# Attention, soft routing and a dense expert block in one kernel: new places for the routing steps, head sums added up pair by pair, and two weight blocks loaded during the attention

## The chip, the cores and the metric

One core of a Trainium2 chip runs the whole program in one launch. The metric is the device time in microseconds (us), the median of the runs shown. Engines are named as the profile names them: PE (TensorE; PEld are its weight loads), DVE (VectorE), ACT (ScalarE), POOL (GpSimd), SP (SyncE, which issues all DMAs here, in its program's order).

## What is computed

```python
def reference(q, k, v, phi, w1, w2, w_in, w_out, s, b):
    # 8 batches, 8 heads, 576 positions, head size 64
    scores = q @ k.T / 8, masked by blocks of 64 (a row block sees the blocks up to its own)
    x = (softmax(scores) @ v)                     # as 4608 tokens x 512
    logits = x @ phi                              # phi 512 x 32
    d = softmax of logits over the tokens         # per slot
    slot_input = d.T @ x                          # 32 slots, 4 for each of 8 experts
    slot_out = relu(slot_input[e] @ w1[e]) @ w2[e]    # w1 8x512x1024, w2 8x1024x512
    x = (softmax of logits over the slots) @ slot_out
    return (s * relu(x @ w_in) ** 2 + b) @ w_out  # w_in 512x2048, w_out 2048x512, float64 words
```

## The kernel before

The program has three stages. **Attention** takes 32 pairs of heads (8 batches of 4 pairs), one after the other. For a pair `p`, `rough` computes rounded scores in four parts r0 to r3, and `rough_max` takes from them, on DVE, the row maxima over blocks of 64 keys; `rough_join` joins two maxima of each row and `m_row` turns them into a row that SP copies into `mr`. Then `score` (four chunks s0 to s3) computes the exact scores in PSUM, `expo` the exponentials `pc` (ACT), `key_sum` adds them up into `S` (POOL, on DVE in the last pair), `sum_hi` and `sum_lo` split `S` into two fp16 parts `sh` and `sl`, `pv` multiplies by V, `tokens` turns the result to tokens and multiplies by phi (tile `tp`, with only one buffer), `dens` sums the denominators into the same tile, and `norm` writes the normalised tokens and their part of the logits to `XB` (4 tiles of 128 tokens) and `XT` (the last 64 tokens of a batch).

The score tiles `s` in PSUM form a ring of two: a part of `rough` or a chunk of `score` can be written only when the tile before the last was read by its `expo` or `rough_max`. r3 of the next pair shares the tile of s1, and the two readers of that tile, `expo` of chunk 1 and `rough_max` of r3, wait for each other in program order.

After each fourth pair a **routing** of the batch runs between the steps of the next pair. `route_s0` sums the logits of the eight heads (the helper `head_sum`, a reduction on DVE), `route_p` transposes them (PE) and takes their running maximum, `route_l` exponentiates (ACT), `route_e` transposes back, `route_x` multiplies by the tokens and adds to `acc`. All of these share `tp` with `tokens`, which waits for the last of them. The last batch's routing has nothing beside it; `slot_inputs` then writes `slotT`.

The **expert stage** multiplies by w1 and w2, 32 blocks of 1 MB each loaded in two halves of 512 KB (`load_w`). Its blocks lie in ten places: four `wlate` and four `wpost` in the memory that the attention's tiles leave, two `wright` in that of the routing's tiles. A place is loaded anew when `used` tells that its block was multiplied. Beside it DVE and ACT convert `w_out` from 64-bit words (`split_wo`). The **dense stage** follows, and the change does not touch it.

What sets the order of the work in the first two stages is the table `SLOT`: each step of a pair has a time in units of an eighth of a pair, every step is put into the plan at `8 * p` plus that time, and the sorted plan is written out engine by engine. So a number of the table decides only which instructions stand before which on an engine's queue. V tiles `RV` have three buffers and are loaded some two pairs ahead (`ld_v`).

Of the kernel before, what the change touches and what calls it, by code (L numbers as in the profile page):

```python
# [10 lines left out]
F32 = mybir.dt.float32  # L11
# [23 lines left out]
}  # L35

ON = {"k": "A", "q": "A", "sl": "D"}
# [6 lines left out]
def fused_kernel(  # L44
# [34 lines left out]
    wpre = wholes(ctx, "wpre", NPRE)  # L79

# [12 lines left out]
    wt = {}  # L93

# [48 lines left out]
    XB = rtp.tile([128, 4, 8, 96], F32, name="xb", bufs=1)  # L143
    XT = rtp.tile([128, 8, 96], F32, name="xt", bufs=1)
# [9 lines left out]
    KT, QT, RV = [None] * 3, [None] * 3, [None] * 3  # L154
    for i in (2, 0, 1):
        KT[i] = earlyp.tile([128, 640], F32, name=f"kt_{i}")
        QT[i] = earlyp.tile([128, 640], F32, name=f"qt_{i}")
        RV[i] = earlyp.tile([128, 5, 128], F32, name=f"rv_{i}")
# [3 lines left out]
    NB_ = {"pc": 5, "mT": 4, "ssp": 1}  # L162
# [12 lines left out]
    MM = [latep.tile([128, 2, 5, 2], F32, name=f"mm_{i}") for i in range(2)]  # L175
# [7 lines left out]
    def build_rest():  # L183
        for d in MX:
            POOL.memset(d.bitcast(F32), 0.0)
        for d in MM:
            POOL.memset(d, -3.0e38)
        POOL.memset(EX[32:64, 128:256], 0.0)
# [100 lines left out]
    def rough_max(p, r):  # L289
        ps = st.pop(("rps", p, r))  # L290
        mm, me = MM[p % 2][:, :, :, 0], MM[p % 2][64:128, :, :, 1]
        by64 = ps[64:128].rearrange("p h (u c) -> p h u c", c=64)
# [9 lines left out]
        else:  # L302
            rmax(me[:, :, 0:1], ps[64:128, :, 448:512])

    def rough_join(p):
        rmax(MX[p % 2][:, 0:10], MM[p % 2].rearrange("p h j a -> p (h j) a"))

# [44 lines left out]
    def key_sum(p, c):  # L352
# [4 lines left out]
        if p == NP - 1 and c == 3:  # L357
            sh, sl = st["s3"] = [ring("s" + x, [128, 2, 576], F16)[:, :, 0:256] for x in "hl"]
# [29 lines left out]
    def pv(p, c):  # L388
        if c == 0:
            st["last"] = st["pv", p] = ps_v.tile([128, 2, 512], F32, tag="pv", name="pv")  # L390
        pc, rv = st["pc", p, c], RV[p % 3]
# [42 lines left out]
    def norm(p):  # L434
# [5 lines left out]
        if p == NP - 1:  # L440
# [3 lines left out]
        DVE.tensor_tensor(out=XB[:, :, 2 * j:2 * j + 2, :], in0=ps[:, :, 0:384].rearrange("p h (u c) -> p u h c", u=4),  # L444
                          in1=rr[:, 0:4].to_broadcast([128, 4, 2, 96]), op=ALU.mult)

        DVE.tensor_tensor(out=XT[l0:l0 + 64, 2 * j:2 * j + 2, :], in0=ps[64:128, :, 384:480],
                          in1=rr[64:128, 4].to_broadcast([64, 2, 96]), op=ALU.mult)
# [13 lines left out]
    def head_sum(o, x):  # L462

        DVE.tensor_reduce(out=o, in_=x, axis=AX, op=ALU.add)  # L464

    def route_s0(b, j0=0, j1=8):

        if b == NB - 1:
            n = 0 if j0 == 0 else 1
            if n == 0:  # L470
                st["part"] = [rtp.tile(x, F32, tag=t, name=t, bufs=1)
                              for t, x in (("partx", [128, 4, 32, 2]), ("partt", [128, 32, 2]))]
            w, v = st["part"]
            head_sum(w[:, :, :, n], XB[:, :, j0:j1, 64:96].rearrange("p u h n -> p u n h"))
            head_sum(v[:, :, n], XT[:, j0:j1, 64:96].rearrange("p h n -> p n h"))
            if n == 0:
                return
            g = lgs[:, gt(b):gt(b) + 5, :]
            DVE.tensor_tensor(out=g[:, 0:4], in0=w[:, :, :, 0], in1=w[:, :, :, 1], op=ALU.add)
            DVE.tensor_tensor(out=g[:, 4], in0=v[:, :, 0], in1=v[:, :, 1], op=ALU.add)  # L480
            return
        head_sum(lgs[:, gt(b):gt(b) + 4, :], XB[:, :, :, 64:96].rearrange("p u h n -> p u n h"))
        if b % 2:
            head_sum(lgs[:, gt(b) + 4, :], XT[:, :, 64:96].rearrange("p h n -> p n h"))

# [49 lines left out]
    def route_x(b):  # L535
# [5 lines left out]
        if b % 2:  # L541
            PE.matmul(ps[0:32, :], d[:, 128:160], XT[:, :, 0:64], start=False, stop=True)
# [5 lines left out]
    def route_s(b):  # L548
# [28 lines left out]
    for p in range(NP):  # L577
# [30 lines left out]
        A("norm", norm)  # L608
        A("mr", m_row)
    for b in range(NB):  # L610
        z = 8 * (4 * b + 3) + O["route"]
        if b == NB - 1:
            at(8 * (NP - 1) + O["den"] + 0.001, 8, route_s0, b, 0, 6)
            at(z + O["rh"], 8, route_s0, b, 6, 8)
        else:
            at(z + O["rh"], 8, route_s0, b)
# [643 lines left out]
```

## Time and profile before

| | |
|---|---|
| median of 3 runs (lowest, highest) | 843.72 us (843.55, 844.74) |
| the profiled execution | 841.7 us |
| its span in the profile | 839.9 us |
| busy share of the span: PE, DVE, ACT, POOL | 93%, 81%, 70%, 26% |
| attention and last routing, expert stage, dense stage | up to about 379 us, 379 to 443, 443 to the end |

The profile shows one execution. Its page has, among others, the span cut into 40 slices of 21 us with the busy share of each engine, the clock that TensorE was granted and the share of the DMA engines; the trace behind it gives for each instruction its start, its duration and what it waited for. A chain of waits is followed back from the last instruction and names at each moment the one thing that was being waited for.

### The profile page before, as it was taken

The numbers are of one execution on the slowest core, as the hardware profiler recorded it, in microseconds if no ns is written. First come the engines' busy times: TensorE is split into PE (matmuls) and PEld (weight loads), VectorE is DVE, ScalarE is ACT, GpSimd is POOL, SyncE is SP. The second block draws the span as 40 slices with busy tenths as digits, with TensorE's granted clock in tenths as the row PEclk, the third lists the DMA queues.
The fourth block names the chain that finished last, engine by engine and source line by source line (L and its number), as shares of the span: only waits on it lengthen the run. The fifth ranks groups of instructions, "written<-read, shape, count | busy, mean of one in ns | idle before, by whom it ended". The sixth has DMA issues, their size and how long they took to land.

```text
span 839.9 us, 18427 instructions
## 1 busy us (share of the span) xinstructions
PE 780.2 (93%) x7604; PEld 580.5 (69%) x7604; DVE 681.7 (81%) x1175; ACT 585.3 (70%) x848; POOL 220.2 (26%) x191
## 2 busy tenths in 40 slices
PE   4999989898989899967888889999999999999996
PEld 3666757575667575732314678888888888888885
DVE  5788888888888888669876788888888888888885
ACT  4766767575767666547876787777777877877771
POOL 3553534443535344402000011111111111111110
PEclk9999999999999999988899999999999999999999
DMA  4565543242434433299990000000000000000001
GB/s 144 196 211 181 196 145 96 81 159 101 157 133 146 146 96 96 82 385 407 397 392 9 1 26 27 26 27 26 27 26 27 26 27 26 27 26 27 26 27 51
DMA packets 40483, 92.97 MB, mean 111 GB/s; under 512 B 4624, under 2 KB 4944, under 8 KB 40400
## 3 DMA queue, kind: packets, MB, share of 16 engines
q1 hardware_dynamic: 40400, 91.80, 31.3%
q8 instruction: 60, 0.98, 0.5%
q14 instruction: 23, 0.19, 0.1%
HBM read 81.86 MB, written 9.44 MB: 109 GB/s over the span
## 4 chain that ended last, share of the span: by engine, by line
PE 77%; DVE 10%; DMA 8%; ACT 3%; issue 1%; POOL 1%; SPq 0%; POOLq 0%; DVEq 0%; ACTq 0%
PE s L343 13%; PE o L1121 13%; PE o L1123 12%; PE o L1122 12%; PE pv L397 9%; PE tp L415 4%; DMA w<-in_moe_w_dram 4%; PE s L286 4%; PE h L1084 4%; DMA w2h<-in_moe_w_dram 3%; DVE mm L272 3%; DVE lgs L464 2%; PE tp L428 2%; ACT rhl L1102 1%; PE hp L922 1%
## 5 line engine op out<-in xcount | busy, mean ns | idle before, releaser
L272 DVE TENSOR_REDUCE mm<-s 64x4 f32<-64x256 f32 (+5 forms) x224 | 139.1, 634 | 50.2 <-ACT pc L350 30.1
L1103 DVE TENSOR_TENSOR rhl<-G,rhl 128x1792 f16<-128x1792 f32 (+1 forms) x76 | 146.2, 1923 | 3.1 <-ACT rhl L1102 2.7
L350 ACT ACTIVATE pc<-s 128x896 f32<-128x896 f32 (+1 forms) x128 | 104.0, 838 | 58.7 <-PE s L343 30.4
L1085 ACT ACTIVATE r<-h 128x512 f32<-128x512 f32 x144 | 85.8, 596 | 60.8 <-PE h L1084 60.8
L343 PE MATMUL s<-qt,kt 64*128 64x448 f32 (+4 forms) x768 | 124.5, 416 | 1.2 <-DVE mm L272 0.5
L1102 ACT CAST rhl<-G 128x1792 f16<-128x1792 f32 (+1 forms) x76 | 121.0, 1592 | 5.4 <-DVE G L1095 5.3
L365 POOL TENSOR_TENSOR S<-pc 128x896 f32<-128x896 f32 x31 | 64.9, 2093 | 181.8 <-ACT pc L350 181.8
L1123 PEld LDWEIGHTS <-rhl 128*128 128x128 f16 x1008 | 98.8, 98 | 13.2 <-DVE rhl L1103 1.6
L1121 PEld LDWEIGHTS <-rhl 128*128 128x128 f16 x1008 | 98.8, 98 | 13.2
L1122 PEld LDWEIGHTS <-rhl 128*128 128x128 f16 x1008 | 98.8, 98 | 11.8
L397 PE MATMUL pv<-pc,rv 128*64 128x448 f32 (+4 forms) x768 | 100.3, 397 | 0.0
L371 POOL TENSOR_TENSOR S<-S,pc 128x640 f32<-128x640 f32 (+2 forms) x93 | 93.3, 1003 | 7.3
L343 PE MATMUL s<-mr,neg 64*128 64x448 f32 (+4 forms) x384 | 94.9, 487 | 0.0
L1140 POOL TENSOR_TENSOR z<-u,bdif 128x256 f32<-128x256 f32 x18 | 41.8, 2320 | 188.8 <-DVE u L1126 188.8
L1093 DVE TENSOR_TENSOR G<-G 128x512 f32<-128x512 f32 (+1 forms) x76 | 50.5, 665 | 46.5 <-ACT G L1092 46.0
L1092 ACT ACTIVATE G<-r 128x1024 f32<-128x1024 f32 (+1 forms) x76 | 76.9, 1011 | 2.2
L397 PEld LDWEIGHTS pv<-pc,rv 128*64 128x64 f32 x768 | 47.3, 136 | 32.1 <-issue 20.7
L343 PEld LDWEIGHTS s<-qt,kt 64*128 64x128 f32 x768 | 60.4, 188 | 7.4 <-DVE mm L272 2.9
L286 PE MATMUL s<-kr,qr 64*128 64x64 f32 (+4 forms) x384 | 54.0, 348 | 10.2 <-ACT kr L243 7.9
L286 PEld LDWEIGHTS s<-kr,qr 64*128 64x128 f32 x384 | 32.7, 191 | 40.2 <-ACT pc L350 21.1
L1084 PE MATMUL h<-ct,mst 128*128 128x256 f16 x288 | 55.2, 274 | 3.5 <-DVE mst L1049 1.3
L415 PEld LDWEIGHTS tp<-IP,ot 64*128 64x128 f32 x640 | 40.8, 188 | 17.3 <-ACT kr L243 7.3
(302 smaller groups left out, 1787.9 us busy)
## 6 DMA issues: line engine op xcount, KB each, us to landing
w<-in_moe_w_dram SPq DMA_DIRECT2D x36, 512.0 KB
w2h<-in_moe_w_dram SPq DMA_DIRECT2D x28, 512.0 KB
qt<-in_q_dram SPq DMA_DIRECT2D x32, 320.0 KB
kt<-in_k_dram SPq DMA_DIRECT2D x32, 320.0 KB
rv<-in_v_dram SPq DMA_DIRECT2D x32, 320.0 KB
wi<-in_moe_w_in_dram SPq DMA_DIRECT2D x8, 1024.0 KB
wo<-in_moe_w_out_dram SPq DMA_DIRECT2D x8, 1024.0 KB
out_dram<-ob SPq DMA_DIRECT2D x16, 256.0 KB
```

Of the source, the lines that this page charges most:

```text
L272: DVE.tensor_reduce(out=o, in_=i, axis=AX, op=ALU.max)
L286: PE.matmul(ps[:, h, o:o + k1 - k0], qt[a, 128 * j:128 * j + 128], kt[a, k0:k1], start=(n == 0), stop=(n == len(RG[r]) - 1))
L343: PE.matmul(ps[:, h, o:o + c1 - c0], a[r], b[r], start=(n == 0), stop=(n == 1))
L350: ACT.activation(out=pc[:, :, 0:w], in_=st.pop(("ps", p, c))[:, :, 0:w], func=AF.Exp, scale=scale)
L371: eng.tensor_tensor(out=x, in0=x, in1=pc[:, :, o:o + c1 - c0], op=ALU.add)
L397: PE.matmul(st["pv", p][r, x[0], x[1]], rv[:, sl, r], pc[:, h, o:o + c1 - c0], start=head, stop=(sl == 4 or c1 <= 128))
L1084: PE.matmul(hps[:, 256 * o:256 * o + 256], mst[:, 128 * f:128 * f + 128], ct[g], start=True, stop=True)
L1102: ACT.copy(rh, G)
L1103: DVE.tensor_tensor(out=rl, in0=G, in1=rh, op=ALU.subtract)
L1121: PE.matmul(o, rh[:, a, n], bh, start=first, stop=False)
L1122: PE.matmul(o, rh[:, a, n], bl, start=False, stop=False)
L1123: PE.matmul(o, rl[:, a, n], bh, start=False, stop=last)
```

## The change

Six things are changed together.

1. `rough_max` reduces all 128 rows for the second maximum too (before, the lower 64), and `rough_join` masks the upper half with a constant column and takes the larger of two in one instruction.
2. `head_sum` becomes an addition for each pair: in the second, third and fourth pair of a batch DVE adds the logits of the pair's two heads to `LA`. `route_s0` is then one addition of two halves. `XT` becomes the fifth tile of `XB`.
3. `SLOT` has new numbers. V is loaded one pair ahead, into two buffers.
4. Two places (`wearly`) of their own hold the first two blocks of w1, loaded in the pairs 26 and 27. Only two `wlate` places remain, so there are ten places as before.
5. `keep_busy` issues products of 128x128 that nobody reads, 10, 3 and 3 of them, between the steps of the last routing.
6. The clearing of `slotT` goes from DVE to POOL, and some rings are smaller (`ot`, `mT`, the conversion's tile `ag`).

```diff
 SLOT = {
-    "ld_k": -20.09325, "ld_q": -20.15856, "ld_v": -11.10707, "rd_k": -14.81079, ...
+    "ld_k": -17.68370, "ld_q": -17.95831, "ld_v": 1.95502, "rd_k": -12.42489, ...
...
-    XB = rtp.tile([128, 4, 8, 96], F32, name="xb", bufs=1)
-    XT = rtp.tile([128, 8, 96], F32, name="xt", bufs=1)
+    XB = rtp.tile([128, 5, 8, 96], F32, name="xb", bufs=1)
+    LA = rtp.tile([128, 5, 2, 32], F32, name="la", bufs=1)
...
-    NB_ = {"pc": 5, "mT": 4, "ssp": 1}
+    NB_ = {"pc": 5, "ot": 1}
...
-        t = {"k": KT, "q": QT, "v": RV}[nm][p % 3]
+        t = {"k": KT, "q": QT, "v": RV}[nm][p % (2 if nm == "v" else 3)]
...
-        mm, me = MM[p % 2][:, :, :, 0], MM[p % 2][64:128, :, :, 1]
-        by64 = ps[64:128].rearrange("p h (u c) -> p h u c", c=64)
+        mm, me = MM[p % 2][:, 0], MM[p % 2][:, 1]
+        by64 = ps.rearrange("p h (u c) -> p h u c", c=64)
...
     def rough_join(p):
-        rmax(MX[p % 2][:, 0:10], MM[p % 2].rearrange("p h j a -> p (h j) a"))
+        mm, me = (MM[p % 2][:, n].rearrange("p h j -> p (h j)") for n in range(2))
+        DVE.scalar_tensor_tensor(out=MX[p % 2][:, 0:10], in0=me, scalar=mlow[:, 0:1], in1=mm, op0=ALU.add, op1=ALU.max)
...
-    def head_sum(o, x):
-
-        DVE.tensor_reduce(out=o, in_=x, axis=AX, op=ALU.add)
...
+    def head_sum(p):
+
+        b, j = p // 4, p % 4
+        if j == 0:
             return
...
+        n = 4 + b % 2
+        x = XB[:, 0:n, 2 * j:2 * j + 2, 64:96]
+        eng = {"P": POOL, "D": DVE}["D" if p == NP - 1 else ON["hs"]]
+        eng.tensor_tensor(out=LA[:, 0:n], in0=XB[:, 0:n, 0:2, 64:96] if j == 1 else LA[:, 0:n], in1=x, op=ALU.add)
+
+    def route_s0(b):
+
+        n = 4 + b % 2
+        DVE.tensor_tensor(out=lgs[:, gt(b):gt(b) + n, :], in0=LA[:, 0:n, 0], in1=LA[:, 0:n, 1], op=ALU.add)
...
+    def keep_busy(n):
+
+        ps = rps(NB - 1, True)[:, 1]
+        for _ in range(n):
+            PE.matmul(ps[:, 0:128], idF, idF, start=True, stop=True)
...
+    at(8 * (NP - 1) + O["den"] + 0.0002, 0, keep_busy, 10)
+    at(z + O["rp"] + 0.0002, 9, keep_busy, 3)
+    at(z + O["rx"] + 0.0002, 10, keep_busy, 3)
...
+    early = [split(t) for t in wearly]
+    for i, t in enumerate(early):
+        home["w1", i] = t
+        at(8 * (26 + i), 10, load_w, ("w1", i), t)
...
-    wlate = wholes(ctx, "wlate", 4, reuse_waits="tile")
+    wlate = wearly + wholes(ctx, "wlate", 4 - NEARLY, reuse_waits="tile")
...
-    toload = list(wseq[16:])
+    toload = list(wseq[16 + NEARLY:])
...
-    at(8 * (NP - 1) + O["norm"] + 0.02, 9, DVE.memset, slotT, 0.0)
+    at(8 * (NP - 1) + O["norm"] + 0.02, 9, POOL.memset, slotT, 0.0)
```

The order of the instructions, not their times, at three places. In a row stand the line, the operation, what it writes and reads, and the size of what it writes. The first place is PE's queue in the pair after the second batch (`kr` and `qr` are `rough`'s operands, `lgs` and `ex` the routing's). Before:

```order
L286 MATMUL s<-kr_130,qr_132 128x512 x2
L313 MATMUL tp<-idF,lgs 128x64 x2
L494 MATMUL tp<-idF,lgs 32x64 x2
L397 MATMUL pv<-pc,rv_136 64x448 x2
L397 MATMUL pv<-pc,rv_136 64x320 x2
...
L286 MATMUL s<-kr_130,qr_132 128x320 x2
L313 MATMUL tp<-idF,ex 128x64 x2
L521 MATMUL tp<-idF,ex 128x64
L343 MATMUL s<-qt_138,kt_137 128x448 x2
L343 MATMUL s<-mr_144,neg 128x448 x2
L539 MATMUL tp<-xb,d 32x512 x4
```

The same place in the changed program:

```order
L311 MATMUL s<-kr_136,qr_138 128x512 x2
L424 MATMUL pv<-pc,rv_145 64x448 x2
L339 MATMUL tp<-idF,lgs 128x64 x2
L516 MATMUL tp<-idF,lgs 32x64 x2
L424 MATMUL pv<-pc,rv_145 64x320 x2
...
L339 MATMUL tp<-idF,ex 128x64 x2
L543 MATMUL tp<-idF,ex 128x64
L311 MATMUL s<-kr_136,qr_138 128x192 x2
L311 MATMUL s<-kr_136,qr_138 128x320 x2
L561 MATMUL tp<-xb,d 32x512 x4
L564 MATMUL tp<-xb,d 32x512
```

The transposes of the logits now stand behind chunk 1 of `pv`, those of the exponentials ahead of r2, and `route_x` ahead of s0. Nothing else moves on PE in the attention.

The second place is DVE's queue at the same point. Before (`mm` and `mx` are the row maxima, `mb` and `nrun` the routing's):

```order
L272 TENSOR_REDUCE mm_162<-s 64x2
L439 TENSOR_SCALAR rs_164<-tp 128x10
L443 RECIPROCAL rr<-rs_164 128x10
L444 TENSOR_TENSOR xb<-tp,rr 128x4x192
L447 TENSOR_TENSOR xt<-tp,rr 64x192
L272 TENSOR_REDUCE mx_160<-mm_162 128x10
L464 TENSOR_REDUCE lgs<-xb 128x128
L464 TENSOR_REDUCE lgs<-xt 128x32
L272 TENSOR_REDUCE mm_161<-s 128x2
L272 TENSOR_REDUCE mm_161<-s 64x2x2
L497 TENSOR_REDUCE mb<-tp 128x1
```

And changed (`la` is the running head sum, `ag` and `wi` belong to the conversion of `w_in`):

```order
L297 TENSOR_REDUCE mm_168<-s 128x2
L663 SCALAR_TENSOR_TENSOR ag<-ag,wi_596 128x512
L332 SCALAR_TENSOR_TENSOR mx_166<-mm_168,mlow 128x10
L665 SCALAR_TENSOR_TENSOR wi_596<-wi_596,ag 128x512
L466 TENSOR_SCALAR rs_171<-tp 128x10
...
L479 TENSOR_TENSOR xb<-tp,rr 64x192
L501 TENSOR_TENSOR la<-la,xb 128x320
L297 TENSOR_REDUCE mm_167<-s 128x2
L297 TENSOR_REDUCE mm_167<-s 128x2x2
L506 TENSOR_TENSOR lgs<-la 128x160
L519 TENSOR_REDUCE mb<-tp 128x1
```

The reductions over eight heads are gone. The maximum of r3 and the join stand ahead of the norm, and in half of the pairs both steps of a conversion do too. The addition that completes the logits stands behind the maxima of r1.

The third place is SP's queue at the end of the attention. Before:

```order
L239 DMA rv_142<-in_v_dram 128x640
L107 DMA wo_4565<-in_moe_w_out_dram 128x2x1024
L325 DMA mr_144<-mT 1x5x128 x2
L113 DMA w2h<-in_moe_w_dram 128x1024 x8
L113 DMA w_4_0_4915<-in_moe_w_dram 128x1024
```

And changed:

```order
L351 DMA mr_149<-mT 1x5x128 x2
L126 DMA wo_4556<-in_moe_w_out_dram 128x2x1024
L264 DMA rv_145<-in_v_dram 128x640
L351 DMA mr_150<-mT 1x5x128 x2
L264 DMA rv_148<-in_v_dram 128x640
L132 DMA w2h<-in_moe_w_dram 128x1024 x4
L132 DMA w_4_0_4925<-in_moe_w_dram 128x1024
```

V of the last pair now stands behind the last `mr`, and four halves (two blocks) instead of eight stand ahead of the first `wpost` place, `w_4_0`.

## Rows read from the trace of the kernel before

**Rows 1.** The page's 40 slices: DMA engines' busy share in tenths

```profile
DMA  4565543242434433299990000000000000000001
```

**Rows 2.** Chain of waits, the same step in three pairs: start us, us, what

```profile
309.55 2.10 PE pv L397 x20
...
319.45 2.10 PE pv L397 x20
...
343.20 2.10 PE pv L397 x20
```

**Rows 3.** Waits of PE from 20 to 356 us: us in total, times, longest

```profile
PE tp L313 <- DVE lgs L464: 7.7, 7, 1.1
PE tp L415 <- DVE acc L544: 6.7, 7, 1.0
```

**Rows 4.** Chain of waits in the pair after the seventh batch

```profile
325.18 0.93 ACT pc L350
...
326.13 0.30 DVE mm L272
...
328.45 1.85 DVE lgs L464
...
332.25 1.15 DVE mm L272
...
335.73 0.76 DVE acc L544
...
336.62 1.36 PE tp L415 x20
```

**Rows 5.** DVE, 20 to 356 us, by form: x count | busy us, mean ns

```profile
L258 DVE TENSOR_TENSOR sl<-pc,sh 128x256 f16<-128x256 f32 x31 | 13.2, 426 | 1.3 <-ACT sh L376 1.0
L636 DVE SCALAR_TENSOR_TENSOR ag<-ag,wi 128x512 int32<-128x512 int32 x16 | 10.9, 683 | 0.0
L464 DVE TENSOR_REDUCE lgs<-xt 128x32 f32<-128x256 f32 x3 | 1.8, 596 | 0.0
```

**Rows 6.** POOL, whole span, by form

```profile
L365 POOL TENSOR_TENSOR S<-pc 128x896 f32<-128x896 f32 x31 | 64.9, 2093 | 181.8 <-ACT pc L350 181.8
L371 POOL TENSOR_TENSOR S<-S,pc 128x640 f32<-128x640 f32 x31 | 48.1, 1551 | 2.4
L1140 POOL TENSOR_TENSOR z<-u,bdif 128x256 f32<-128x256 f32 x18 | 41.8, 2320 | 188.8 <-DVE u L1126 188.8
```

**Rows 7.** Instructions in order of time, PE, POOL and DVE in pair 30

```profile
351.32 0.97 PE L397 MATMUL pv<-pc,rv 128*64 128x448 f32 x4
...
352.10 3.22 POOL L371 TENSOR_TENSOR S<-S,pc 128x640 f32<-128x640 f32 x3
353.21 0.71 DVE L258 TENSOR_TENSOR sl<-pc,sh 128x256 f16<-128x256 f32 x1 [1.03 <-ACT sh L376]
```

**Rows 8.** Instructions in order of time, SP at the attention's end

```profile
354.44 1.84 SPq L113 DMA_DIRECT2D w2h<-in_moe_w_dram  x4
363.38 0.80 SPq L113 DMA_DIRECT2D w2h<-in_moe_w_dram  x2
```

**Rows 9.** Chain of waits: last routing, a product for `roots`, the last weights

```profile
366.54 1.02 DVE slotT L676
...
373.73 1.87 PE s L539 x8
...
387.36 0.33 PE roots L820 x2
...
431.91 10.38 DMA w2h<-in_moe_w_dram
```

**Rows 10.** Stretches: PE, PEld, DVE, ACT, POOL busy us; granted clock, DMA share, GB/s

```profile
369.50:370.00 0.50, 0.00 (x0) 0.00 (x0) 0.47 (x3) 0.00 (x0) 0.00 (x0) 0.52 1.03 393
438.00:440.00 2.00, 1.61 (x8) 0.29 (x8) 0.00 (x0) 0.00 (x0) 0.00 (x0) 1.00 1.05 408
```

**Rows 11.** Chain of waits at the start: from a K load's issue to its landing

```profile
7.95 3.24 DMA kt<-in_k_dram
```

More of the change, by code (lines that the diff above doesn't have):

```diff
@@ L93, in fused_kernel, with __init__, __getitem__, tile @@
     wt = {}
+    class split:
+        def __init__(self, pool):
+            self.pool, self.t = pool, None
+        def __getitem__(self, h):
+            if h == 0:
+                self.t = self.pool.tile([128, 2048], F32, tag="w", name="w2h")
+            t = self.t
+            class place:
+                def tile(_, shape, dt, tag, name):
+                    return t[:, 1024 * h:1024 * h + 1024]
+            return place()
     def words(key, q0, q1):
@@ L157, in fused_kernel @@
         QT[i] = earlyp.tile([128, 640], F32, name=f"qt_{i}")
-        RV[i] = earlyp.tile([128, 5, 128], F32, name=f"rv_{i}")
+        if i == 2:
+            AG = earlyp.tile([128, 512], I32, name="ag")
+        else:
+            RV[i] = earlyp.tile([128, 5, 128], F32, name=f"rv_{i}")
     MR = [earlyp.tile([128, 640], F32R, name=f"mr_{i}") for i in range(2)]
@@ L173, in fused_kernel @@
     MX = [latep.tile([128, 128], F32R, name=f"mx_{i}") for i in range(2)]
-    MM = [latep.tile([128, 2, 5, 2], F32, name=f"mm_{i}") for i in range(2)]
+    MM = [latep.tile([128, 2, 2, 5], F32, name=f"mm_{i}") for i in range(2)]
+    mlow = const.tile([128, 1], F32, name="mlow")
     RS = [latep.tile([128, 10], F32, name=f"rs_{i}") for i in range(2)]
@@ L187, in build_rest @@
             POOL.memset(d, -3.0e38)
+        POOL.memset(mlow, 0.0)
+        POOL.memset(mlow[0:64], -3.0e38)
         POOL.memset(EX[32:64, 128:256], 0.0)
@@ L357, in key_sum @@
         if p == NP - 1 and c == 3:
-            sh, sl = st["s3"] = [ring("s" + x, [128, 2, 576], F16)[:, :, 0:256] for x in "hl"]
+            t = ring("S", [128, 2, 448], F32).rearrange("p h c -> p (h c)").bitcast(F16)
+            sh, sl = st["s3"] = [t[:, 512 * x:512 * x + 512].rearrange("p (h c) -> p h c", h=2) for x in range(2)]
             ACT.copy(sh, pc[:, :, 0:256])
@@ L443, in norm @@
         DVE.reciprocal(out=rr.rearrange("p u h a -> p (u h a)"), in_=r)
-        DVE.tensor_tensor(out=XB[:, :, 2 * j:2 * j + 2, :], in0=ps[:, :, 0:384].rearrange("p h (u c) -> p u h c", u=4),
+        DVE.tensor_tensor(out=XB[:, 0:4, 2 * j:2 * j + 2, :], in0=ps[:, :, 0:384].rearrange("p h (u c) -> p u h c", u=4),
                           in1=rr[:, 0:4].to_broadcast([128, 4, 2, 96]), op=ALU.mult)
-        DVE.tensor_tensor(out=XT[l0:l0 + 64, 2 * j:2 * j + 2, :], in0=ps[64:128, :, 384:480],
-                          in1=rr[64:128, 4].to_broadcast([64, 2, 96]), op=ALU.mult)
+        xt = XB[l0:l0 + 64, 4, 2 * j:2 * j + 2, :]
+        if ON["xt"] == "A":
+            for h in range(2):
+                ACT.activation(out=xt[:, h], in_=ps[64:128, h, 384:480], func=AF.Copy, scale=rr[64:128, 4, h, :])
+        else:
+            DVE.tensor_tensor(out=xt, in0=ps[64:128, :, 384:480], in1=rr[64:128, 4].to_broadcast([64, 2, 96]), op=ALU.mult)
         for c in range(4):
@@ L541, in route_x @@
         if b % 2:
-            PE.matmul(ps[0:32, :], d[:, 128:160], XT[:, :, 0:64], start=False, stop=True)
+            PE.matmul(ps[0:32, :], d[:, 128:160], XB[:, 4, :, 0:64], start=False, stop=True)
         f = st["rl", b]
@@ L608, in fused_kernel @@
         A("norm", norm)
+        A("hs", head_sum)
         A("mr", m_row)
@@ L733, in fused_kernel @@
     ready, summed, todo, active = set(), set(), [], []
-    toload = list(wseq[16:])
-    class split:
-        def __init__(self, pool):
-            self.pool, self.t = pool, None
-        def __getitem__(self, h):
-            if h == 0:
-                self.t = self.pool.tile([128, 2048], F32, tag="w", name="w2h")
-            t = self.t
-            class place:
-                def tile(_, shape, dt, tag, name):
-                    return t[:, 1024 * h:1024 * h + 1024]
-            return place()
+    toload = list(wseq[16 + NEARLY:])
     def advance():
@@ L865, in paced @@
         return int(min(n, 8) * CFIRST + max(n - 8, 0) * CLATE)
-    empty = wpost[::-1] + [split(t) for t in wlate[::-1]]
+    empty = wpost[::-1] + [split(t) for t in wlate[:NEARLY - 1:-1]]
     with tc.manual_schedule():
```

38 lines of the change are left out of this document (9 added, 29 removed), and 14 rows, old and new, of the table SLOT.

## The prediction

> **What bounds the kernel now.** I read the page's slices first. The DMA row [rows 1] stands at 9 in only four slices, the 18th to the 21st (about 357 to 441 us): the expert stage moves weights without a pause. The chain of waits agrees: it runs through the weights' DMAs to 431.91 + 10.38 = 442.3 us [rows 9], while the conversions on DVE and ACT are over at 438 us, where the stretch shows both at 0.00 [rows 10]. So that stage ends when the last bytes have come. The dense stage behind it is not touched, and I cost it at nothing.
>
> In the attention the chain lies on PE. One step of `pv` comes back after 319.45 - 309.55 = 9.90 us in a plain pair, but two pairs with a routing in them take 343.20 - 319.45 = 23.75 [rows 2], 3.95 more than two plain ones. The list of what PE waited for names the reason [rows 3]: 7.7 us for the logits and 6.7 for `acc`, seven times each, 14.4 in all. The chain inside such a pair [rows 4] then shows where these waits are made: from 326.13 to 332.25 + 1.15 = 333.40 us DVE works without a gap, and 1.85 of it is the reduction over the heads. A routing is bound by DVE's queue, a plain pair by PE.
>
> **The routings.** The order of the changed program and the rows of this pair [rows 4] give, for an even batch:
> - The maximum of r3 no longer waits for `expo` of chunk 1 (that one waits for it now), so it starts at 325.18 and ends 0.30 later, at 325.5. `expo` then ends at 326.45.
> - Join and norm take what lay between 326.43 and 328.45: 2.0, to 327.5.
> - The head sum replaces 1.85 us. An addition with 256 elements in a row took 0.43 [rows 5]; I take that also for 320 (scaled with the elements it would be 0.53). But POOL's first addition of `S` (2.09 [rows 6]) starts when `expo` ends and lasts to 328.55, and I let the head sum wait for it (reason below): it ends at 329.0.
> - The maxima of r1, the completing addition, the transposes and `mb` with `nrun` took 332.25 - 330.30 = 1.95 with no addition and no PE in between; I add 0.6 for these: 331.55. The maximum of r0 (1.15) ends at 332.7, 0.7 before 333.40.
> - `d` (0.3) leads to `route_x`, which now stands ahead of s0, at 333.05. It took 1.04, to 334.1. On DVE the maxima of r2, some 1.75, stand ahead of `acc`: 334.8, and 0.76 for `acc`: 335.55. `tokens` starts there instead of at 336.62, a gain of 1.1.
>
> The four even batches give 4.4. In the three odd ones a second reduction (0.60 [rows 5]) goes too: 1.7 each, 5.1. In the pairs 4, 8, 16 and 20, four of these seven, two conversion steps of 0.68 [rows 5] now stand ahead of the norm; about half a microsecond of each gain goes, 2.0. **Gain 7.5** of the 14.4. Bounds: all of it, and nothing, should the new order wait elsewhere.
>
> **The plain pairs.** 24 head sums of 0.43 are 10 us of DVE, beside PE's 9.90 a pair, where DVE has a tenth or more free. What they may wait for is POOL. In pair 30 one subtraction on DVE, both of whose inputs lie in SBUF, started inside POOL's additions and took 0.71 instead of 0.43 [rows 7, 5]: POOL's first, of 1.55 [rows 6], started at 352.10 and ended about 353.6, and the subtraction ended at 353.92. So it waited for one addition of POOL and then had its turn. The head sum has two such inputs and falls into POOL's first addition in each pair: up to 1 us of wait, behind which stand the maxima of r1. PE has written r1 only some 0.2 us before, so without conversions nothing reaches PE. In the 8 plain pairs with conversions ahead of a head sum r1 and r0 are read about 0.7 late, and s0, which needs r0's buffer, waits 0.3. **Cost 2.4.** Bounds: 0 (POOL yields) and the rival below. The Trainium skill, SBUF — State Buffer, "Who interferes with whom", says that a VectorE instruction with two SBUF inputs contends with a GpSimd instruction that reads SBUF, that whoever issues first has the shared ports for its whole instruction, and that the other fully blocks. Taken alone it speaks against this part, because the reduction that went, with a single input, would not contend. Our one row agrees; by the rule each sum may lose more than one turn, and that is the first rival.
>
> The maxima over all 128 rows have the elements of before in each row: 0. V is issued behind `mr`. In pair 30 `pv` began at 351.32 [rows 7], and the first issue behind `mr` came at 354.44 [rows 8], 3.1 us later. A K load took 3.24 us to land [rows 11]; where a block of 1 MB stands ahead (ten pairs) 2.6 more, and some 0.9 for its issue: 9.8 of 9.9. In the other pairs there are 3 us to spare. I cost it at 0, with V not late, and bound it by 1.5 in ten pairs. The start gets two small memsets and another order on ACT: **cost 0.3**, between 0 and 1.
>
> **The last routing.** The clearing of `slotT` (1.02 [rows 9]) and the reductions leave DVE: logits about 1.3 us earlier. The granted clock fell in the stretch 369.5 to 370 (0.52 [rows 10], the lower of the levels 1.2 and 2.4 GHz) after PE had idled there; `route_x` then took 1.87 for what took 1.04 earlier [rows 9, 4]. With the idle products between, I let the clock stay: 2 us in all steps. The ten products take 10 x 0.33 = 3.3 at the price of the product for `roots` [rows 9], and the gap they fill is 2.9, so they may cost 0.4. All this, some 3 us, I cost at **nothing**: the weights' DMAs run beside it. If that cover were gone (the two `wright` places wait for `route_x`), I put 1 us on what would show.
>
> **The early blocks.** Two blocks are 2.1 MB, at 408 GB/s [rows 10] 5.1 us less in the stage bound by DMA. But ahead of the place that waits for the last `pv` (issue at 363.38 [rows 8]) stood three blocks and now stand two, so the queue runs dry sooner: behind that point only one block less is to come, 2.6. That place now also waits for DVE's `sl`, ahead of which the order puts a norm and a head sum: about 0.9 later. In return no place waits for the norm's last step any more; I put 0.7 on that, an estimate between 0 and the 0.9 just named. **Gain 2.4**, between 0 and 5.1.
>
> **Sum.** 7.5 - 2.4 - 0.3 + 2.4 = 7.2 us less: 841.7 - 7.2 = 834.5 for the profiled execution. The median of the runs shown is 2.0 above that execution, so 843.7 - 7.2 = **836.5**.
>
> **The rivals.**
> - *POOL goes first.* If the head sum loses two turns, POOL's 1.55 us [rows 6] come on top: r1 and r0 are read 1.5 later and s0 waits about 1.2 in 24 pairs, 29 us, and the routings' gain is gone with it. With 2.4 from the early blocks: 843.7 + 29 - 2.4 = about 870. For it: POOL's three additions follow each other closely, and `z`, with 256 elements, took 2.32 us where 640 took 1.55 [rows 6], so one engine does hold up the other. Against it: the one DVE row waited for a single addition [rows 7]. It decides once DVE loses the second turn. Chance 0.08.
> - *V comes late.* With one pair's lead and a block ahead, ten pairs wait 1.5 us: 836.5 + 15 = about 851. For it: the margin of 0.1 above. Against it: K's 3.24 was measured behind other transfers. Chance 0.05.
> - *All waits go.* The routings hide entirely (14.4) and the early blocks count in full (5.1): 843.7 - 19.5 = 824. Half of that way counts here too, 824 to 831. Against it: `lgs` now stands behind r1's maxima. Chance 0.17.
> - *It changes nothing to speak of.* The routings gain 3 instead of 7.5 and the early blocks 0: within 842.0 and 845.4. Chance 0.08. That the clock falls in spite of the idle products is a part of the forecast, since the DMAs cover it.
>
> **The numbers.** The forecast, 831 to 842, has 0.62. A measurement can tell about 0.2% (1.7 us) from no change. Faster: 0.62 + 0.17 = 0.79; same 0.08; slower 0.08 + 0.05 = 0.13. The range of 827 to 843 leaves out the slower cases and the far end of the fastest.
>
> **What would show it.** Right: PE's waits for the logits and for `acc` together at 5 to 8 us instead of 14.4; plain pairs at 9.9 us, some 10.2; the last DMA of the weights about 8 us earlier than 442; a head sum of 0.4 to 1.4 us beside POOL. Wrong: plain pairs above 10.5, PE waiting for V, or an expert stage that ends later after its start.

## The result, and the profile after the change

The changed kernel takes **832.69 us** (median of 4 runs, 831.40 to 834.36) beside 843.95 for the kernel before; the ratio is 0.9868, with a 95% interval from 0.9854 to 0.9881. The forecast was 836.5, in a range of 827 to 843. The profiled execution has a span of 830.5 us, 9.4 less than 839.9.

What PE waited for between 20 and 345 us (us in total, times, longest) answers to [rows 3]:

```profile
PE tp L339 <- DVE lgs L506: 3.4, 7, 0.7
PE tp L339 <- ACT ex L533: 1.0, 3, 0.4
PE pv L424 <- DMA rv<-in_v_dram: 0.9, 1, 0.9
PE tp L561 <- DVE d L549: 0.8, 3, 0.3
PE tp L561 <- DVE d L547: 0.2, 1, 0.2
```

The 14.4 us for the logits and for `acc` have become 3.4; `acc` is not waited for at all. The chain of waits (start us, us, what) answers to [rows 2, 4, 9]:

```profile
300.09 2.10 PE pv L424 x20
...
309.93 2.10 PE pv L424 x20
...
319.41 1.29 DVE mm L297 x2
320.70 0.21 DVE lgs L506
...
321.85 1.14 DVE mm L297
...
323.27 1.07 PE tp L561 x8
324.33 1.16 PE s L369 x6
325.49 1.26 PE tp L442 x20
...
332.00 2.10 PE pv L424 x20
...
420.91 10.73 DMA w2h<-in_moe_w_dram
```

A plain pair takes 9.84 us (309.93 - 300.09; before 9.90), two with a routing in them 22.07 instead of 23.75. DVE's reduction of 1.85 us is gone from the path. The weights' last DMA ends at 431.64, before at 442.29.

The instructions in order of time (start us, us, engine, what, in brackets the idle time before and what ended it) show the attention's first and last `pv`, the one V that came late, a head sum beside POOL, and SP at the attention's end:

```profile
21.96 0.97 PE L424 MATMUL pv<-pc,rv 128*64 128x448 f32 x4
...
189.25 0.97 PE L424 MATMUL pv<-pc,rv 128*64 128x448 f32 x4 [0.87 <-DMA rv<-in_v_dram]
...
316.90 2.10 POOL L392 TENSOR_TENSOR S<-pc 128x896 f32<-128x896 f32 x1 [4.26 <-ACT pc L376]
318.00 1.28 DVE L501 TENSOR_TENSOR la<-la,xb 128x256 f32<-128x256 f32 x1
319.08 3.22 POOL L398 TENSOR_TENSOR S<-S,pc 128x640 f32<-128x640 f32 x3
320.62 0.28 DVE L506 TENSOR_TENSOR lgs<-la 128x128 f32<-128x128 f32 x1
...
343.55 1.85 SPq L132 DMA_DIRECT2D w2h<-in_moe_w_dram  x4
349.08 0.60 PE L424 MATMUL pv<-pc,rv 128*64 128x448 f32 x2
352.90 12.55 SPq L132 DMA_DIRECT2D w<-in_moe_w_dram  x12
```

The head sum started at 318.00 inside POOL's first addition and ended 0.28 after that one's end (316.90 + 2.10 = 319.00): it waited for one turn. Over the eight additions of this form the mean is twice the 0.43 that an addition of this size took alone [rows 5] (DVE, 20 to 345 us, by form: x count | busy us, mean ns), while the completing addition and the new join lost nothing to speak of:

```profile
L501 DVE TENSOR_TENSOR la<-la,xb 128x256 f32<-128x256 f32 x8 | 7.1, 889 | 0.3
L332 DVE SCALAR_TENSOR_TENSOR mx<-mm,mlow 128x10 fp32r<-128x10 f32 x31 | 7.0, 227 | 0.5
L506 DVE TENSOR_TENSOR lgs<-la 128x128 f32<-128x128 f32 x4 | 1.2, 299 | 0.0
```

Where the 9.4 us came from, by the starts of every pair's first `pv` in the order of time (before 21.13 to 360.42, after 21.96 to 349.08):

| stretch | before, us | after, us | difference |
|---|---|---|---|
| start to the first `pv` | 21.1 | 22.0 | +0.8 |
| the seven pairs with a routing | 102.1 | 90.8 | -11.3 |
| the other pairs up to the last | 237.2 | 236.3 | -0.9 |
| last pair's first `pv` to the last weights | 81.9 | 82.6 | +0.7 |
| dense stage | 397.6 | 398.8 | +1.2 |

So the attention gave 11.4 us, the weights' stage did not become shorter with two blocks fewer to load, and the untouched dense stage gave back 1.2. The stretches (us, busy us of PE, PEld, DVE, ACT, POOL; granted clock, DMA share, GB/s) show why for both:

```profile
351.50:354.00 2.50, 1.90 (x30) 1.59 (x26) 2.25 (x4) 1.48 (x3) 0.00 (x0) 1.00 0.17 43
...
356.00:360.00 4.00, 4.00 (x26) 3.73 (x25) 2.52 (x7) 0.00 (x0) 0.00 (x0) 0.69 1.00 384
...
474.00:478.00 4.00, 2.92 (x15) 2.12 (x15) 2.46 (x3) 3.28 (x7) 0.55 (x1) 0.57 0.00 0
478.00:482.00 4.00, 4.00 (x24) 2.95 (x23) 3.93 (x6) 1.83 (x2) 2.22 (x1) 0.58 0.01 4
```

From 351.5 to 354 the DMAs were nearly dry: the two blocks that stood ahead had landed, and SP waited until 352.90 for the last pair (7.4 us, for DVE's `sl`). What that costs shows in the same view taken from that issue to the last weights, before (from 363.38 [rows 8]) and after:

```profile
363.38:442.30 78.92, 60.92 (x453) 20.31 (x453) 62.63 (x127) 55.97 (x85) 4.95 (x7) 0.89 1.01 389
...
352.90:431.64 78.74, 64.61 (x485) 24.48 (x481) 59.08 (x121) 55.29 (x83) 4.57 (x4) 0.93 0.99 374
```

Before, 29 blocks were still to come at that point, and after, 28: one block less took only 0.2 us less, at 374 GB/s on average instead of 389. In the dense stage the granted clock was low (1.2 GHz) for some 6.8 us (4 x 0.86 + 4 x 0.84, worked out from 0.57 and 0.58). At the same place of the stage in the kernel before it was low for 3.4:

```profile
484.00:488.00 4.00, 2.27 (x12) 1.61 (x12) 2.81 (x3) 3.28 (x7) 0.55 (x1) 0.70 0.00 0
488.00:492.00 4.00, 4.00 (x34) 3.36 (x33) 3.59 (x5) 2.91 (x4) 1.57 (x1) 0.88 0.00 0
```

### The profile page after: what moved, and what is told of

The parts are those of the page before. It is cut to its first block, busy times and chain, and to the rows that moved or that the text cites. A ratio compares the mean times of both kernels' runs of the same rounds, so it can differ in the third digit from the quotient of the medians.

```text
span 830.5 us, 18462 instructions
## 1 busy us (share of the span) xinstructions
PE 784.3 (94%) x7636; PEld 584.8 (70%) x7636; DVE 676.8 (82%) x1190; ACT 581.9 (70%) x848; POOL 226.2 (27%) x194
## 4 chain that ended last, share of the span: by engine, by line
PE 79%; DVE 8%; DMA 7%; ACT 2%; issue 1%; POOL 1%; SPq 1%; POOLq 0%; DVEq 0%; ACTq 0%
PE s L369 13%; PE o L1134 13%; PE o L1136 13%; PE o L1135 13%; PE pv L424 9%; PE tp L442 4%; PE s L311 4%; PE h L1097 4%; DMA w<-in_moe_w_dram 3%; DMA w2h<-in_moe_w_dram 3%; DVE mm L297 2%; PE tp L455 2%; DMA rv<-in_v_dram 1%; ACT rhl L1115 1%; PE hp L935 1%
## 5 line engine op out<-in xcount | busy, mean ns | idle before, releaser
L297 DVE TENSOR_REDUCE mm<-s 128x4 f32<-128x256 f32 (+5 forms) x224 | 130.5, 629 | 41.7 <-PE s L311 37.7
L392 POOL TENSOR_TENSOR S<-pc 128x896 f32<-128x896 f32 x31 | 67.7, 2182 | 166.0 <-ACT pc L376 166.0
L398 POOL TENSOR_TENSOR S<-S,pc 128x640 f32<-128x640 f32 (+2 forms) x93 | 95.4, 1026 | 7.3
L369 PEld LDWEIGHTS s<-mr,neg 64*128 64x128 f32 x384 | 39.4, 189 | 15.1 <-issue 10.4
```

What stands on the lines that cost most here:

```text
L297: DVE.tensor_reduce(out=o, in_=i, axis=AX, op=ALU.max)
L369: PE.matmul(ps[:, h, o:o + c1 - c0], a[r], b[r], start=(n == 0), stop=(n == 1))
L398: eng.tensor_tensor(out=x, in0=x, in1=pc[:, :, o:o + c1 - c0], op=ALU.add)
```

## The experiments

The open questions were what made the routings shorter (the sums, the order, or both), what a head sum costs beside POOL, and where the early blocks' gain went. Each ratio is to the kernel before on the same chip; four runs (the sums on POOL, the other addresses, V ahead of the blocks, both) come from a second chip, on which the kernel before took 844.56 us.

**The old reductions in the new order.**

```diff
 def head_sum(p):
+    return
...
 def route_s0(b):
-    DVE.tensor_tensor(out=lgs[:, gt(b):gt(b) + n, :], in0=LA[:, 0:n, 0], in1=LA[:, 0:n, 1], op=ALU.add)
+    DVE.tensor_reduce(out=lgs[:, gt(b):gt(b) + n, :], in_=XB[:, 0:n, :, 64:96].rearrange("p u h n -> p u n h"), axis=AX, op=ALU.add)
```

> The changed kernel with the head sums of the pairs undone: the routing reduces over all eight heads in one instruction, at the new place behind the maxima of r1. If the logits' way through DVE is what bounds a routing, each routing loses what the reduction (1.94 us for 128 results a row, some 2.4 for 160) costs over the addition of two halves (0.30 and 0.43): 4 x 1.6 + 3 x 2.0 = 12 us, so about 845 us, and the pairs with a routing go back from about 12.3 and 13.9 to about 13.9 and 15.9. If the new order alone carries the gain, under 3 us are lost: at most 836. In both cases the plain pairs tell what the 24 head sums cost beside POOL: by the forecast they get shorter than 9.83 where conversions stand ahead (0.3 in 8 pairs, 2.4 in all), if the sums are hidden they stay at 9.83.

Measured: 852.69 us, ratio to the kernel before 1.0105 (1.0088 to 1.0123). The new order with the old reductions is slower than the kernel before. The waits of PE and two kinds of stretches of this run:

```profile
PE tp L339 <- DVE lgs L505: 16.0, 7, 2.5
```

```profile
64.50:66.50 2.00, 0.05 (x2) 0.00 (x0) 1.97 (x2) 0.00 (x0) 1.64 (x3) 1.00 0.41 109
...
68.00:69.00 1.00, 1.00 (x12) 0.85 (x10) 0.60 (x1) 0.11 (x1) 0.00 (x0) 0.50 1.03 377
69.00:70.00 1.00, 1.00 (x12) 0.69 (x8) 0.29 (x1) 0.69 (x3) 0.00 (x0) 0.50 1.03 401
```

PE waits 16.0 us for the logits instead of 3.4: 12.6 more, the 12 of the expectation. But the attention (first to last `pv`) is 19.5 us longer. The rest lies in the clock: PE was idle from 64.5 to 66.5, and then the granted clock stood at 0.50. That happened in six of the seven pairs, after gaps of 2.1 to 2.5 us; in the last one the clock stayed up behind a gap of 2.1. `acc` is waited for no more in this run either, but for 6.6 us in the two runs below that keep the old table: that part of the gain is the order's. The plain pairs tell the other half: without head sums, 23 of them took 227.5 us, and with them 227.3. **The sums cost the plain pairs nothing that shows.**

**Products in the wait.** The same kernel, with six products nobody reads ahead of the routing's transposes:

```diff
 def route_p(b):
     ps = rps(b, True)
+    for _ in range(6 if b < NB - 1 else 0):
+        PE.matmul(ps[:, 1, 0:128], idF, idF, start=True, stop=True)
```

> The changed kernel with the reductions over eight heads (as in the first experiment, 852.7 us), and six products of 128x128 that nobody reads ahead of each of the first seven routings' transposes, where PE waited up to 2.5 us for the logits. In the first experiment PE's waits for the logits were 12.6 us longer than in the changed kernel, and its attention 19.9; the granted clock fell to 0.5 for 3.4 us in six of these pairs. If the clock's fall after such a wait makes the other 7.3, it stays at 1.00 here and the time is about 852.7 - 7.3 = 845.4 us, 844 to 848 with what the products take themselves. If the fall has another cause or costs nothing, the clock falls again and the time is 852 to 856.

Measured: 845.71 us, ratio 1.0019 (1.0005 to 1.0032). The same stretches:

```profile
64.50:66.50 2.00, 1.55 (x14) 1.36 (x12) 1.97 (x2) 0.00 (x0) 1.60 (x3) 1.00 0.39 132
...
68.00:69.00 1.00, 0.83 (x16) 0.57 (x16) 0.98 (x3) 0.78 (x4) 0.00 (x0) 1.00 0.98 355
```

The logits come no earlier, but the clock stays at 1.00, and 7.0 us are back. The one pair whose clock had not fallen takes the same as without the products (13.90 and 13.93 us), the six others 1.0 to 1.4 less. So 7 of the 20 us were not the wait but PE at half its clock behind it. Products that nobody reads, 1.6 us of PE in each of seven pairs, paid here because they stood in a wait that was there anyway.

**The sums in the old order.** The kernel before with head sums as in the change (`LA`, the fifth tile of `XB`) and nothing else:

```diff
-    "norm": 11.64578,
+    "norm": 11.64578, "hs": 11.65078,
...
+    A("hs", head_sum)
```

> The kernel before with the running head sums alone: the old table, the old maxima, V two pairs ahead, no early blocks, no idle products; each pair's sum stands right behind its norm, and the routing adds the two halves where the reduction stood. If what PE waits for is DVE's work ahead of the logits, the reduction's 1.94 and 1.85 us become 0.3 to 0.9, and the seven routings gain 1 to 1.6 us each, 7 to 11 in all: 834 to 838 us with PE's wait for the logits near nothing. If the sums pay only with the new order (the sum of the fourth pair, 0.4 to 0.9 us beside POOL, now stands in the same gap, and acc is waited for as before), the gain is under 4: 840 to 845. Plain pairs: 9.90 as before if the sums are hidden, 10.2 and more where POOL's turn reaches PE.

Measured: 843.24 us, ratio 0.9996 (0.9985 to 1.0006): no gain that the runs can tell. DVE by form, and the place in the order of time:

```profile
L475 DVE TENSOR_TENSOR lgs<-la 128x128 f32<-128x128 f32 x4 | 6.1, 1519 | 0.0
...
L470 DVE TENSOR_TENSOR la<-la,xb 128x256 f32<-128x256 f32 x8 | 3.4, 425 | 0.2
```

```profile
327.48 3.38 POOL L371 TENSOR_TENSOR S<-S,pc 128x640 f32<-128x640 f32 x3
...
327.89 1.51 DVE L475 TENSOR_TENSOR lgs<-la 128x128 f32<-128x128 f32 x1
```

Here it is the *completing* addition that loses a turn: it starts 0.4 us into POOL's addition of 1.55 [rows 6] and takes 1.5 instead of 0.3, which is nearly the reduction's 1.9 again. The pairs with an even batch stay at 13.82, those with an odd one go from 15.56 to 15.09. PE's wait for `acc` stays at 6.6. The seven pairs gained 1.6 us in all in this profile; from the last pair's first `pv` to the last weights it took 83.6 us instead of 81.9. The last batch's sums changed there too; whether they are the reason is not shown.

**The new steps by the old table.**

```diff
-    "ld_k": -17.68370, "ld_q": -17.95831, "ld_v": 1.95502, "rd_k": -12.42489, "rd_q": -13.74636, "r0": -9.02522,
+    "ld_k": -20.09325, "ld_q": -20.15856, "ld_v": 1.95502, "rd_k": -14.81079, "rd_q": -18.16397, "r0": -11.18452,
...
+    5.78017, "oc": 6.88883, "den": 10.19669, "norm": 11.64578, "hs": 11.65078, "route": 12.44301, "re": 2.40618, "rp": 0.37853,
...
```

> The changed kernel with the numbers of the old table (V's number is the new one, the head sum stands right behind the norm). If the head sums alone carry the gain of the routings, the time stays within 3 us of the changed kernel, at most 836, with the routing pairs at 12.3 and 13.9. If the order carries part of it, the routing pairs lose about 1 us each and more: 840 and up. The plain pairs tell whether the order took them from 9.90 to 9.83 (then they are back at 9.90) or something else did (9.83).

In this kernel the conversion's single tile `ag` is filled again before its last reader, so `w_in` is computed otherwise. Measured: 860.55 us, ratio 1.0194 (1.0178 to 1.0210). PE's waits and DVE by form:

```profile
PE tp L339 <- DVE mx L332: 22.7, 21, 1.7
```

```profile
L332 DVE SCALAR_TENSOR_TENSOR mx<-mm,mlow 128x10 fp32r<-128x10 f32 x31 | 36.8, 1187 | 0.2
```

A join of 10 results a row, 0.23 us in the new order, takes 1.19: the new join has two inputs in SBUF, where the old reduction had one and took 0.17, and by the old table it starts inside POOL's additions. PE waits for it 21 times. By the expectation this run should have told whether the order carries part of the gain. It shows more. In eight plain pairs the join lost no turn, and these take 9.83 to 9.84 by the old table too; so what made the plain pairs shorter is not the order. And the order decides which of the new instructions falls into POOL's turns, the join here, the completing addition in the run before this, and in the changed kernel the head sum, for which nobody waits.

**The sums on POOL.** In `ON`, `"hs": "P"`.

> The changed kernel with the head sums on POOL instead of DVE. If the place on DVE between the norm and the maxima is what matters, this relieves DVE by 24 x 0.87 us, but POOL's sum stands behind two additions of S (2.2 and 1.6 us), so the logits come later in the routing pairs: 1 to 2 us each, 839 to 846 us, and plain pairs at 9.83. If POOL holds up DVE's maxima and norm in every pair, plain pairs lengthen and the time goes above 846. If POOL has the time, it stays at 831 to 834.

Measured: 857.96 us, ratio 1.0153 (1.0132 to 1.0174).

```profile
PE tp L339 <- DVE lgs L506: 19.5, 7, 3.0
```

On POOL the pair's sum stands behind the additions of `S`, the logits come up to 3.0 us late, and the granted clock falls in all seven pairs with a routing, where the first experiment had it in six. None of the three cases of the expectation came: the waits grew by 16.1 us where I had priced 7 to 14, the clock behind them I had not priced, and the plain pairs did not lengthen by more than 0.7 us in all.

**No early blocks.** `NEARLY = 0`, and `empty` takes all four `wlate`.

> The changed kernel without the two early places: four blocks are loaded in four places behind the last mr, as before the change. By the two traces the stage bound by DMA is as long with 60 halves to load as with 64 (88.1 and 87.9 us), because the queue ran dry at about 351 and waited for the last pv. Then the time stays within 1.5 us of the changed kernel: 831 to 834.5, with no dry stretch at 351 to 354. If the early blocks are worth the 2.4 of the forecast, it is about 835; if their bytes count in full, 838.

Measured: 834.93 us, ratio 0.9890 (0.9876 to 0.9903). That is the expectation's case of about 835, and not the one of no effect, though the last run below puts the changed kernel itself at 834.06. The stretch from 350 to 354 is not dry here (409 GB/s). The profiled execution is 3.0 us longer than the changed kernel's. From the last pair's first `pv` to the last weights it takes 83.8 us, against 82.6 with the early blocks (82.0 in a second profile): they are worth 1 to 2 there, not 5.1. Another 1.6 lie in the attention, where V came late three times (1.7 us of PE's waits). And without them this stretch is 1.9 longer than in the kernel before (81.9), so something else in the change costs time there; V of the last pair, which now stands ahead of the blocks, is one candidate, and no run tests it.

**No idle products.** In `keep_busy`, `range(0)`.

> The changed kernel without the 16 products that nobody reads. By the forecast the last routing is hidden by the weights' DMAs: the granted clock falls for longer there, route_x takes up to 1.9 us instead of 1.06, and the time stays within 1 us of the changed kernel (832 to 834). If the routing's end does set the end of the stage (the place that waits for route_x), it costs 1 to 3 us: 834 to 836.

Measured: 834.58 us (832.91 to 838.05), ratio 0.9888 (0.9867 to 0.9908). It overlaps the changed kernel's interval, so the times settle nothing. The profiles say more: the first product of the last `route_x` and the DMAs behind it, without the idle products and then with them.

```profile
361.63 1.94 PE L561 MATMUL s<-xb,d 128*32 128x512 f32 x8
365.00:367.00 2.00, 1.08 (x9) 0.97 (x8) 0.75 (x1) 1.66 (x2) 0.00 (x0) 1.00 0.62 154
...
361.78 1.06 PE L561 MATMUL s<-xb,d 128*32 128x512 f32 x8 [0.16 <-DVE d L549]
365.00:367.00 2.00, 1.56 (x17) 0.85 (x20) 1.25 (x2) 1.64 (x2) 0.00 (x0) 1.00 0.83 313
```

Without them the granted clock was 0.50 from 358 to 362, `route_x` took nearly twice as long, SP waited 7.0 us for its end instead of 6.0, and the last weights came 84.1 us after the last pair's first `pv` (with them 82.6, and 82.0 in a second profile). In this one execution that is the second case of the expectation: the routing's end reaches the weights. With the products the clock fell beside the first ten in one of the changed kernel's two profiles (0.69 from 356 to 360) and stayed at 1.00 in the other; at `route_x` it was up in both.

**Other addresses for the tiles.** In this run and the two that build on it (both, and the halves swapped) `earlyp` ends behind `ag` and `rv_1`, `latep` follows, and a third pool holds `rv_0`, the other `kt` and `qt`, `mr` and `neg`:

```diff
+            latep = att.enter_context(tc.tile_pool(name="latep", bufs=1))
+            earlyp = att.enter_context(tc.tile_pool(name="freep", bufs=1))
...
-    empty = wpost[::-1] + [split(t) for t in wlate[:NEARLY - 1:-1]]
+    empty = wpost[1::-1] + wpost[:1:-1] + [split(t) for t in wlate[:NEARLY - 1:-1]]
```

> The changed kernel with other addresses alone: the tiles of q, k and mr lie where two of the four places behind the attention are loaded, and these two places are taken first. The order of the instructions is the same on every engine. The first of these places then waits for the pv of pair 30 and for the last score products, which are over at about 349 us, and not for the last pv. If the dry stretch at 351 to 354.5 is what took the early blocks' gain, it goes (2.9 us of DMA time at 410 GB/s) and the stage ends at about 428.7 instead of 431.6: about 830 us. If something else ends the stage (conversions, the routing, the products), the time stays at 832 to 834.

Measured: 832.36 us, ratio 0.9856 (0.9832 to 0.9880). No difference that the runs can tell; in the profile the stretch behind the last pair's first `pv` is 81.5 us, 1.1 and 0.5 shorter than in the changed kernel's two profiles.

**V ahead of the blocks.**

```diff
-    at(8 * (2 + 7 * (4 * i + 3) // 4) + 15 if i < 4 else 120 + 24 * (i - 4), 10, load_w, ("wo", i), home["wo", i])
+    at(8 * (2 + 7 * (4 * i + 3) // 4) + 18 if i < 4 else 123 + 24 * (i - 4), 10, load_w, ("wo", i), home["wo", i])
...
-    at(8 * (26 + i), 10, load_w, ("w1", i), t)
+    at(8 * (26 + i) + 3, 10, load_w, ("w1", i), t)
```

> The changed kernel with the blocks of w_out and the two early blocks issued behind V of the pair instead of ahead of it. V was late once, in the pair after the sixteenth (10.77 us instead of 9.83, PE waited 0.94 for rv), where two blocks stood ahead. That wait goes: 0.9 us less, about 831.8, and all plain pairs at 9.83. If the wait has another cause, it stays and the time is the changed kernel's.

Measured: **830.64 us** (829.32 to 830.75), ratio 0.9825 (0.9806 to 0.9844), the fastest of all. No wait for `rv` is left in its profile; one `mr` came 0.5 late instead, in a pair that took 10.80. So the attention gained nothing there (327.3 us from the first to the last `pv`, in the changed kernel 327.1). The 1.7 us by which its span is shorter lie behind the attention: 0.4 up to the last weights, 1.4 in the dense stage, where the clock was low for 3.4 us instead of 6.8. The runs show that this kernel is faster; that V's place is why, they do not show.

**Both.**

> The other addresses and V ahead of the blocks together. If the two gains are independent (one in the expert stage, one in the attention), 2.9 + 0.9 us less than the changed kernel: about 829 us. If the one takes the place of the other, no less than the better of the two alone.

Measured: 831.30 us, ratio 0.9835 (0.9812 to 0.9859): no better than V alone. Its profile tells where the gain of the addresses went (stretches, then what SP waited for):

```profile
350.00:354.00 4.00, 3.40 (x42) 2.37 (x38) 3.70 (x7) 2.35 (x5) 1.15 (x3) 1.00 1.03 418
...
362.00:364.00 2.00, 1.93 (x11) 1.02 (x9) 0.83 (x2) 2.00 (x3) 0.00 (x0) 1.00 0.31 43
364.00:366.00 2.00, 1.56 (x16) 0.98 (x19) 1.11 (x2) 1.79 (x2) 0.00 (x0) 1.00 0.83 303
```

```profile
SPq L132 <- PE s L565: 5.2, 1, 5.2
```

The dry stretch at 351 is full (418 GB/s), and another has opened at 362: the queue now reaches the places under the routing's tiles before `route_x` (L565) is done. In the changed kernel SP waits 6.0 us at the same place, but loads under way cover it. The last routing is hidden only as long as the queue is late.

**The halves of those places swapped.**

```diff
-    empty += places(ph2, "wright", 2, side="right", reuse_waits="tile")
+    empty += [p[::-1] for p in places(ph2, "wright", 2, side="right", reuse_waits="tile")]
```

> The run with the other addresses and V ahead of the blocks (831.3 us), and in the two places that the routing's tiles leave the halves change their order: the first half then lies where no tile of the routing lies, and does not wait for route_x. In that run the first dry stretch was gone, but the queue ran dry at 362 to 366 us instead, waiting for route_x (5.2 us of SP's time, some 2.6 us of traffic). If this second wait is what took the rest of the gain, one half more (1.28 us) fills it: 830 us, the stage's end at about 428.8 instead of 430.07. If the products of the first expert set the end instead, nothing changes: 831.3.

Measured: 831.73 us, ratio 0.9862 (0.9844 to 0.9880). It did not test what it was made for. The half that waits only for the last score products moved to the head of SP's queue, ahead of the blocks that could have gone at once:

```profile
342.69 0.38 SPq L265 DMA_DIRECT2D rv<-in_v_dram  x1
348.75 0.33 SPq L132 DMA_DIRECT2D w<-in_moe_w_dram  x1
349.13 2.02 SPq L132 DMA_DIRECT2D w2h<-in_moe_w_dram  x4
```

SP stood for six microseconds, and the dry stretch was back, only earlier. With the queue late again, none opened at 362 (410 GB/s from 362 to 366). Whether a half more would fill that one in the run before stays open.

**The changed kernel once more.**

> The changed kernel once more, beside the run with the other addresses and the swapped halves on the same chip: 832.7 us, with V late in one pair or in several, and the dense stage's low clock 3.4 or 6.8 us long. Each such event moves it by about 1 us, so that its runs spread over some 3 us.

Measured: 834.06 us (832.65 to 835.35), ratio 0.9887 (0.9865 to 0.9909). In its profile V was late in two pairs, and the dense stage took 400.1 us. The run with V ahead (829.32 to 830.75) lies below all eight runs of the changed kernel (831.40 to 835.35).

## Why the prediction was right, and where its terms were not

The time lies 3.8 us under the forecast, inside its range, with the sign and the main mechanism right. But the routings' gain was put too low, the plain pairs have a small gain in place of a cost, the early blocks' gain did not come, and the dense stage was missing. That the total came so near is in part luck: laid beside the profile, the attention gave 6.6 us more than the terms for it and what lies behind it 4.3 less. Two of the prediction's own signs of being wrong showed in the small, a wait for V and a stage of the weights that was 0.7 longer, and the waits for the logits and `acc` (3.4) fell below its 5 to 8.

**The routings: right in mechanism, 11.3 instead of 7.5.** The steps worked out for an even batch can be laid beside the pair from 318 us on, 9.59 us earlier than in the prediction (the pair's first `pv` came at 317.97 instead of 327.56). Head sum done: forecast 329.0, measured 319.28 + 9.59 = 328.9. r0's maximum: 332.7, measured 322.99 + 9.59 = 332.6. `route_x` begins: 333.05, measured 332.9. Up to there it holds within 0.2. The step that failed is the last one, "the maxima of r2, some 1.75, stand ahead of `acc`": they took 1.35 and ended at 324.58, so `acc` was over 0.7 earlier than forecast, and `tokens` began at 325.49 + 9.59 = 335.1 behind the products of `score`, not behind `acc`: a gain of 1.5 instead of 1.1. The 2.0 taken off for conversions ahead of the norm in four pairs was too much: these pairs take 12.3 to 12.4 and 13.9 to 14.0, the others 12.2 and 13.8, 0.7 in all.

**The plain pairs: the step "cost 2.4" failed.** That the head sum waits for one addition of POOL and then has its turn is what the traces show (0.89 us on average, 1.28 in the pair shown; forecast 0.4 to 1.4). That it reaches PE is not: with the sums and without them the pairs take the same, so what stands behind them on DVE has at least that much slack. In place of a cost there was a gain of 0.07 a pair, 1.8 in all, less 0.9 for the one V that came late. Where it comes from is not shown: not from the sums (it stays without them, and with them alone a pair takes 9.92), and not from the order (by the old table the pairs without a late join take 9.83 too), which leaves the other new steps. The rule of the Trainium skill (SBUF — State Buffer, "Who interferes with whom"), that the later engine blocks for the other's whole instruction, agrees with the two DVE instructions shown in the order of time that had to wait: they ended 0.3 and 0.4 us behind POOL's addition. That DVE would lose a second turn, the first rival, is in no row.

**The early blocks: the step "gain 2.4" failed.** I saw that the queue would run dry behind two blocks, and put that at one block, so that "only one block less is to come, 2.6". From the issue that ends the dry stretch to the last weights those 2.6 came to 0.2, at the lower average rate shown above. The 0.9 by which that issue comes later was right (3.8 us behind the last pair's first `pv` instead of 3.0), and the 0.7 in return shows in no row. So the stage got 0.7 longer instead. What was left of the dry stretch at that issue (to 354 us at 43 GB/s) is part of the lower rate, and the rest is not explained: without the early blocks, and without the dry stretch, it took 83.8 us and not 81.9. From 399 to 411 us the weights came at about 386 GB/s where the kernel before, as far from its end, had 404 to 407; but so had the sums in the old order, whose stretch was no shorter.

**The last routing at nothing: right, as long as the products stand there.** The forecast that idle products keep the clock up holds for `route_x` (1.06 us in both profiles, 1.94 without them); beside the ten products themselves it fell in one of two. With them the DMAs covered the routing. Without them some 1.5 us showed, and the other addresses opened a gap behind `route_x` in spite of them.

**The start** cost 0.8 instead of 0.3. **The dense stage**, costed at nothing, gave back 1.2: the clock was low there for 6.8 us instead of 3.4. The run with V ahead had it low for 3.4 again and took 397.4, and the changed kernel's second profile took 400.1: this differs between executions that share every instruction of that stage, and was not to be forecast from the change.

**The rival "V comes late"** happened in the small: one pair of ten, 0.9 us instead of 15, in other executions two or three pairs. The margin of 0.1 was real. Moving a number by three eighths of a pair took that wait away, and a late `mr` took its place.

The sum of the profile (0.8 - 11.3 - 0.9 + 0.7 + 1.2 = -9.5) is less than the medians' 11.3, since the profiled execution of the kernel before was 2.2 under its median and that of the changed kernel (832.2) 0.5.

## What to carry to other kernels

Before an instruction with one SBUF input is replaced by a cheaper one with two, look at what GpSimd does at that moment: the same sums were worth nothing that the runs can tell in the old order (843.24 beside 843.7) and 20 us in the new one (832.69 beside 852.69), and the new order without them was slower than the kernel before. When a wait of TensorE grows, price what the clock does behind it as well as the wait; here products that nobody reads, set into the wait, bought that part back. And where a queue runs dry for one reason, look at its next wait before you count the gain: filling one gap opened the other.

## What was not expected of the hardware

- A VectorE join of 128x10 took 1.19 us on average instead of 0.23, and an addition of 128x128 took 1.52 instead of 0.30, for having two SBUF inputs and starting inside a GpSimd addition. The wait depends on what POOL has begun, not on the size of DVE's own work.
- In six of seven pairs a gap of PE of 2.1 to 2.5 us in the middle of the attention was followed by a granted clock of 0.50 for 3.4 us; in the seventh, behind a gap of 2.1, it was not, nor in the kernel before behind two gaps of about 1 us in the same pair. It cost 7 us over six pairs, over a third of what that run lost in the attention.
